# Linear attention and channel mix on one core: the fourth batch's q and the fifth batch's y turned by DMA, loads held behind turning DMAs, and another order table

## The chip, the cores and the metric

The kernel runs on one core of a Trainium2 chip. Its time is device time in microseconds, the median of several runs. Batches are counted from 0 here, as in the code: the fourth batch of q is batch 3, the fifth batch of y is batch 4.

## What is computed

For each of 8 batches and 8 heads of 576 tokens and 64 dimensions: `kv = k^T v`, `out = q kv`, each row of `out` divided by its root mean square and multiplied by `g_norm`. The heads side by side are `x`, 576 x 512 a batch, and then comes a channel mix:

```python
x_prev = x shifted by one token (zeros ahead)
xk = mu_k * x + (1 - mu_k) * x_prev
xr = mu_r * x + (1 - mu_r) * x_prev
k = relu(xk @ w_k)            # 512 x 1024
v = (k * k) @ w_v             # 1024 x 512
out = sigmoid(xr @ w_r) * v   # w_r 512 x 512
```

Inputs and the output are float32; the kernel works in bfloat16 with float32 sums.

## The kernel before, in words

Nothing is scheduled by a compiler. `ORDER` (lines 18 to 110) is a table of words, one step each, and the loop at line 791 records them in this order; every engine runs its own instructions in the order in which the words give them. A word names an operation, batch and part; `'` puts an evacuation or copy on VectorE (DVE) instead of ScalarE (ACT); digits behind `=` choose the PSUM banks. The table has eight periods; period 2 begins with batch 2's `K` steps, and so on.

The steps that matter here, per batch `a`:

- `ld.n.a` (line 189): the load of k, v or q (n = 0, 1, 2), issued by GpSimd (POOL) with a cast to bfloat16, 0.59 MB in SBUF. Odd batches use buffers `in_k`, `in_v`, `in_q`; even ones reuse `sq`, `qT` and `q` of batch 0. Batches 0 and 1 and the weights are loaded ahead of the table (lines 182 to 213 and 689 to 691), batch 1's in two halves.
- `kv.a` (line 278): 72 matmuls on TensorE (PE). `kvo.a` evacuates them. For batch 1 the two halves of the heads are separate words with an `h`: `kvh.0` and `kvh.1` at line 522, `kvho`, `uh`, `sqh`, `redh`, `rsh`, `mulh`, and for the turning back `x0h`, `xh` and `x0ho`, `xho`.
- q has to stand with its dimensions on the partitions. Either `qt.a.0` and `qt.a.1` (line 322) turn it with 72 transposes on PE, and four `qto` evacuate them; or `qd.a` (line 299) issues one transposing DMA on SyncE's (SP's) queue. `QD = 4` (line 293): batches 4 to 7 take the DMA. After a DMA the product `u.a` uses line 316 (`u_turned`) with a second copy of `kv` whose halves are swapped (`kvs.a`), otherwise line 352.
- `sq`, `red`, `nw`, `mul`: squares on ACT, sums and a root by Newton steps on DVE, the product with it on DVE. `nw.a` has 8 small steps.
- y has to be turned back to channels on partitions. Either `x0.a` and `x.a.0.4` (line 435, 36 transposes on PE), evacuated by `x0o` and `xo` with a multiplication by g; or `mul` writes into the single tile `yd`, `yd.a` (line 407) issues one transposing DMA on SP's queue into `xT`, and `gx.a.0`, `gx.a.1` multiply by g in place. `YD = (5, 6, 7)` (line 390).
- `wrap`, `dif`, `sc`, `add`: the token shift and the mix; `add.a.0.*` completes `xk`, `add.a.1.*` completes `xr`.
- `K.a.fc.h` (line 631): four matmuls of 288 columns and a relu into `rt`; `ks` squares it into `sqk`. For batches 0 and 1 these are `Ka`, `Kz`, `Kp` and `ksp`.
- `R.b.t` (line 653): four matmuls of 512 columns and a sigmoid. `V.b.t.part` (line 663): four matmuls of 512 columns; `Vq` is a half of that, two matmuls, with part 0 to 3. R, V and the steps after them go over a pair of batches in 9 tiles of 128 tokens, t = 0 to 8.
- `fin.b.t` (line 676): DVE's product of the two, then two stores on SP's queue. `fip` and `sta` split the stores of the last tiles over SP's and ACT's queues. `L.part` (line 671): the last tile in two column halves.
- `wm.n`: n matmuls on zeros whose result is not used. `tab`: the load of ACT's table with the sigmoid.

Buffers: `work` tiles of one tag rotate (`rt` has 7 places, `sig` 6, `out` 7).

Of the kernel before, what the change touches and what calls it, by code (L numbers as in the profile page):

```python
# [9 lines left out]
FP32 = mybir.dt.float32  # L10
# [9 lines left out]
    cast.0' cast.1' kvc.0.2=01 kvco.1' kvco.0 qtc.0.2=23 qtco.1' cols=4 qtco.0 wm.1.0=1 uc.1=5 sqc.1 uc.0=6  # L20
    qtc.2.2=70 qtco.3' msc.1=1 sqc.0 msc.0=3 qtco.2' rsc.1 wm.1.1=0 kvc.2.1=4 kvco.2 wm.1.2=1 uc.4=2 rsc.0 mcc.1
    uc.2=0 wm.1.3=5 kvc.3.1=7 mcc.0 sqc.2 kvco.3' sqc.4 difh.0.0.256.576 sc.0.0.1.256.576' msc.2=1 uc.3=4
    sc.0.0.0.256.576' uc.5=5 sqc.3 msc.4=3 wm.1.4=7 msc.3=6 rsc.2 add.0.0.0.256.576 wm.1.5=7 Ka.0.4=7 Ka.0.5=1
    rsc.3 mcc.2 mcc.3 dih.0.2.256.576 dih.0.3.256.576 sqc.5 rsc.4 Ka.0.3=6 msc.5=0 fu.0.0.2.256.576 Ka.0.2=4
# [13 lines left out]
    mulh.1.0.1 Vq.0.0.0=3 xho.2.2.1.1 mulh.1.1.1 Vq.0.0.1 xho.2.2.1.0 dif.1.384.576 sc.1.0.2.384.576'
    sc.1.0.1.384.576' Vq.0.0.2 sc.1.0.3.384.576 Vq.0.0.3 sc.1.0.0.384.576' adda.1.0.384.576 xh.0.2.1=07
    xho.0.2.1.1' x0h.1=46 x0ho.1.1' xho.0.2.1.0 wrap.1 x0ho.1.0 dif.1.0.384 sc.1.0.3.0.384' Vq.0.3.3  # L40
    sc.1.0.0.0.384' ld.1.3 Vq.0.1.3 tab sc.1.1.3' R.0.1=0 fin.0.1 Kp.1.0.3=4 Kp.1.0.2=7 sc.1.0.2.0.384'
    add.1.0.1.0.384 Kp.1.0.0'=6 sc.1.1.1 Kp.1.0.1'=0 R.0.0=4 sc.1.0.1.0.384' add.1.0.0.0.384 ld.0.3 R.0.2=7
    kv.2=26 ksp.1.0.0.8 fin.0.0 Kp.1.1.2=4 Kp.1.1.0=0 Kp.1.1.5=7 kvo.2.0 sc.1.1.0' Kp.1.1.1=3 qt.2.1=40
    sc.1.1.2' ksp.1.1.0.2 kvo.2.1 add.1.1.0 qto.2.1.1 qt.2.0=72 R.0.3=3 qto.2.0.1' add.1.1.1 Kp.1.1.3=2
    Kp.1.1.6=6 qto.2.1.0' qto.2.0.0' fin.0.2 fin.0.3 u.2.0=40 sq.2.0.1 ksp.1.1.2.4' Kp.1.1.4'=7 u.2.2=3 u.2.1=25
    sq.2.0.0 sq.2.2.0 sq.2.1.1 red.2.5.9 sq.2.1.0 red.2.0.5 Kp.1.1.7=6 ksp.1.1.4.6 nw.2.0.1 nw.2.1.2 R.1.6=1
    nw.2.2.3 nw.2.3.4 nw.2.4.5 ld.2.4 R.1.7=7 ld.0.4 nw.2.5.6 nw.2.6.7 nw.2.7.8 R.1.8=6 mul.2.0.1 mul.2.2.0
# [8 lines left out]
    K.2.0.1'=5 K.2.1.1=2 K.2.3.1=6 sq.3.0.1 add.2.1.1 red.3.0.5 red.3.5.9 nw.3.0.1 nw.3.1.2 nw.3.2.3 K.2.6.0=5
    nw.3.3.4 R.2.1=2 ld.2.6 R.2.3=6 nw.3.4.5 K.2.1.0=5 K.2.3.0=2 V.1.8.0=6 nw.3.5.6 nw.3.6.7 K.2.6.1=5 V.1.8.1
    ks.2.1 nw.3.7.8 mul.3.1.0 K.2.5.0=2 mul.3.1.1 mul.3.0.1 mul.3.0.0 mul.3.2.0 K.2.2.0=5 K.2.0.0=1 kv.4=02
    ks.2.0' kvo.4.0 fin.1.8 x.3.0.4=75 x0.3=41 K.2.7.0=3 K.2.5.1=0 kvo.4.1 ks.2.2 ks.2.3' x0o.3.1' xo.3.0.4.1'
    kvs.4.1' R.2.2=6 wrap.3 K.2.4.1=1 xo.3.0.4.0' x0o.3.0' dif.3 sc.3.0.3' sc.3.0.2' sc.3.1.2' K.2.4.0=3 ld.0.6  # L60
# [7 lines left out]
    K.3.0.0=2 nw.4.4.5 K.3.5.1=6 ks.3.4 ld.1.7 nw.4.5.6 kvs.5.0' nw.4.6.7 nw.4.7.8 R.3.6=7 K.3.1.0=2 K.3.0.1=6
    K.3.1.1=7 kvs.5.1' ks.3.5 mul.4.1.0 ks.3.2 mul.4.0.0 K.3.6.1=2 K.3.3.1=6 mul.4.2.0 mul.4.1.1 R.3.7=7
    V.2.3.0=3 mul.4.0.1 ks.3.6' ks.3.0 V.2.3.1 ks.3.3' ks.3.1 x0.4=40 fin.2.3 x0o.4.0 x.4.0.4=25 u.5.2=6  # L70
    u.5.1=71 x0o.4.1' xo.4.0.4.1' u.5.0=43 xo.4.0.4.0 V.3.6.0=0 sq.5.0.1 sq.5.0.0 sq.5.2.0 wrap.4 sq.5.1.0 dif.4
    sc.4.0.3 V.3.6.1 fin.3.6 red.5.5.9 sq.5.1.1 red.5.0.5 V.3.5.0=5 R.3.5=2 nw.5.0.1 nw.5.1.2 sc.4.0.0 qd.6
# [14 lines left out]
    add.5.1.0 K.5.3.1=6 K.5.4.1=1 nw.6.7.8 K.5.6.0=4 mul.6.0.1 mul.6.2.0 mul.6.1.0 V.4.1.0=6 kv.7=13 kvo.7.1'
    mul.6.0.0 ks.5.5 mul.6.1.1 sc.5.1.2 ks.5.0 kvo.7.0' K.5.7.1=4 kvs.7.1' K.5.2.0=0 kvs.7.0' ks.5.2 yd.6
    ks.5.3' sc.5.1.3 ks.5.4 V.4.1.1 V.4.3.0=7 ks.5.1' u.7.2=3 u.7.0=54 u.7.1=20 V.4.3.1 ks.5.6' sq.7.0.0
    add.5.1.1 sq.7.0.1 sq.7.2.0 fin.4.1 sq.7.1.0 sq.7.1.1 fin.4.3 K.5.7.0=1 ks.5.7' red.7.0.5 R.5.5=6 R.5.8=7  # L90
    red.7.5.9 R.5.4=1 nw.7.0.1 nw.7.1.2 R.5.7=6 V.5.7.0=7 V.5.8.0=1 nw.7.2.3 nw.7.3.4 gx.6.1' nw.7.4.5 nw.7.5.6
# [734 lines left out]
```

## Time and profile before

| | us |
|---|---|
| median of 3 runs (198.97 to 199.28) | 199.24 |
| the profiled execution, its own time | 198.45 |
| its span, first to last instruction | 196.7 |
| TensorE busy | 185.8 |
| DVE busy | 163.0 |
| ACT busy | 134.1 |
| POOL busy | 27.6 |

The span is what the profile's tables are measured in; the profiled execution's own time has 1.75 us more around it. The transposing DMAs before the change, as SP issued them: q of batch 4 at 63.0, of batch 5 at 77.1, of batch 6 at 103.6 and of batch 7 at 118.9; y of batch 5 at 111.9, of batch 6 at 135.4 and of batch 7 at 149.8. POOL issued the loads of batch 3 from 28.6 to 31.3, of batch 4 from 46.3 to 48.5, of batch 5 from 57.7 to 59.9, of batch 6 from 75.4 to 77.6 and of batch 7 from 92.0 to 94.3.

How to read it: a line of a group or of the timeline gives start or busy time, engine, line of the kernel, what is written and read, and in square brackets how long the engine stood idle before it and what ended that. A window gives the busy time of each engine in a stretch, in the order PE, PEld (weight loads), DVE, ACT, POOL, then the granted share of TensorE's clock, the share of the 16 DMA engines, and GB/s.

### The profile page before, as it was taken

How to read it: one execution, taken by the hardware profiler on the slowest of the kernel's cores; microseconds unless marked ns; L12 is line 12 of the kernel's file. 1: busy time of each engine (PE TensorE's matmuls, PEld its weight loads, DVE VectorE, ACT ScalarE, POOL GpSimd, SP SyncE). 2: the span in 40 equal slices, each digit the busy share in tenths (PEclk: the TensorE clock that was granted, in tenths of full speed). 3: DMA queues.
4: the chain of work that ended last, by engine and by line, in shares of the span. 5: the costliest groups of instructions: out<-in, count | busy, mean ns of one | idle time of the engine just before them, and what ended most of it. 6: DMA issues, size and time to landing. Idle time of an engine off the chain costs nothing.

```text
span 196.7 us, 5776 instructions
## 1 busy us (share of the span) xinstructions
PE 185.8 (94%) x2387; PEld 111.1 (56%) x2409; DVE 163.0 (83%) x356; ACT 134.1 (68%) x275; POOL 27.6 (14%) x44
## 2 busy tenths in 40 slices
PE   7788899999999999999999999999999999999991
PEld 2435565665564667567554775676445666764450
DVE  2488899996999999978999899899899997876241
ACT  2375898779969867969987658989855557532310
POOL 7953343004021004002100000000000000000000
PEclk9999999999999999999999999999999999999999
DMA  5999999999999998999999378335723842005654
GB/s 212 219 211 206 202 205 208 207 217 243 230 230 208 220 189 223 224 170 268 154 215 202 81 136 171 86 80 29 176 45 58 182 107 57 0 0 130 140 144 124
DMA packets 38030, 31.51 MB, mean 160 GB/s; under 512 B 18924, under 2 KB 32500, under 8 KB 38004
## 3 DMA queue, kind: packets, MB, share of 16 engines
q0 software_dynamic: 14400, 16.19, 49.3%
q1 hardware_dynamic: 23204, 14.43, 33.5%
q10 hardware_dynamic: 400, 0.52, 0.8%
q8 instruction: 19, 0.31, 0.6%
q14 instruction: 7, 0.06, 0.1%
HBM read 33.56 MB, written 9.44 MB: 219 GB/s over the span
## 4 chain that ended last, share of the span: by engine, by line
PE 80%; DVE 9%; DMA 4%; issue 2%; ACT 2%; SPq 0%; DVEq 0%; POOLq 0%
PE ps_v L663 28%; PE ps_km L631 28%; PE ps_r L653 15%; DMA q<-in_q_dram 3%; PE ps_kv L287 2%; PE ps_u L316 1%; DVE y L420 1%; PE ps_x L435 1%; DMA out_dram<-out_sb 1%; DVE xT L512 1%; DVE out_sb L676 1%; PE ps_u L352 1%; DVE ss L361 1%; DVE sqk L639 1%; PE ps_qt L330 1%
## 5 line engine op out<-in xcount | busy, mean ns | idle before, releaser
L663 PE MATMUL ps_v<-wv_sb,sqk 128*128 128x512 bf16 x266 | 64.8, 379 | 1.0 <-issue 0.3
L631 PE MATMUL ps_km<-xk,wk_sb 128*128 128x288 bf16 (+3 forms) x480 | 64.0, 285 | 0.0
L631 PEld LDWEIGHTS <-wk_sb 128*128 128x128 bf16 x480 | 45.7, 98 | 16.2
L663 PEld LDWEIGHTS <-sqk 128*128 128x128 bf16 x280 | 26.7, 98 | 29.5 <-issue 0.6
L623 ACT ACTIVATE rt<-ps_km 128x288 bf16<-128x288 f32 (+3 forms) x81 | 33.5, 427 | 12.6 <-PE ps_km L631 9.0
L653 PE MATMUL ps_r<-wr_sb,xr 128*128 128x512 bf16 x136 | 34.9, 379 | 0.5
L656 ACT ACTIVATE sig<-ps_r 128x512 bf16<-128x512 f32 x36 | 21.2, 596 | 18.9 <-PE ps_r L653 18.6
L676 DVE TENSOR_TENSOR out_sb<-ps_v,sig 128x512 f32<-128x512 f32 (+1 forms) x37 | 24.3, 670 | 9.3 <-PE ps_v L663 7.7
L637 ACT ACTIVATE sqk<-rt 128x576 bf16<-128x576 bf16 (+4 forms) x32 | 23.4, 746 | 4.4 <-DVE rt L625 4.2
L601 ACT ACTIVATE m<-dx,cols 128x576 bf16<-128x576 bf16 (+1 forms) x30 | 21.7, 756 | 4.2 <-DVE dx L595 4.0
L625 DVE TENSOR_SCALAR rt<-ps_km 128x288 bf16<-128x288 f32 (+3 forms) x39 | 17.8, 473 | 6.6 <-PE ps_km L631 5.0
L653 PEld LDWEIGHTS <-xr 128*128 128x128 bf16 x144 | 13.9, 98 | 14.2
L361 DVE TENSOR_REDUCE ss<-sq 128x16 f32<-128x1024 bf16 (+1 forms) x12 | 15.8, 1344 | 0.4 <-ACT sq L357 0.4
L357 ACT ACTIVATE sq<-ps_u 128x512 bf16<-128x512 f32 (+1 forms) x30 | 14.6, 556 | 0.0
L618 DVE TENSOR_TENSOR xr<-m,xT 128x1152 bf16<-128x1152 bf16 x16 | 11.9, 750 | 0.8 <-ACT m L601 0.8
L639 DVE TENSOR_TENSOR sqk<-rt 128x576 bf16<-128x576 bf16 (+3 forms) x25 | 11.7, 482 | 0.7 <-ACT rt L623 0.6
L595 DVE TENSOR_TENSOR dx<-xT 128x2304 bf16<-128x2304 bf16 (+5 forms) x13 | 11.4, 893 | 0.4
L603 DVE TENSOR_SCALAR m<-dx,cols 128x576 bf16<-128x576 bf16 (+3 forms) x36 | 11.4, 346 | 0.2
L618 DVE TENSOR_TENSOR xk<-m,xT 128x1152 bf16<-128x1152 bf16 (+2 forms) x16 | 10.9, 699 | 0.2
L420 DVE TENSOR_TENSOR y<-ps_u,rs 128x512 bf16<-128x512 f32 (+1 forms) x15 | 8.4, 628 | 0.1
L217 ACT CAST kv<-ps_kv 128x128 bf16<-128x128 f32 (+1 forms) x15 | 3.3, 244 | 6.9 <-PE ps_kv L472 5.7
L261 PE MATMUL ps_warm<-zeros 128*128 128x512 bf16 x18 | 6.9, 502 | 1.2 <-DVE eps L224 1.2
(91 smaller groups left out, 162.2 us busy)
## 6 DMA issues: line engine op xcount, KB each, us to landing
out_dram<-out_sb SPq DMA_DIRECT2D x67, 128.0 KB, 3.2
qT<-in_v_dram POOLq DMA_DIRECT2D x3, 576.0 KB, 14.4
sq<-in_k_dram POOLq DMA_DIRECT2D x3, 576.0 KB, 12.9
q<-in_q_dram POOLq DMA_DIRECT2D x3, 576.0 KB, 10.8
in_q<-in_q_dram POOLq DMA_DIRECT2D x3, 576.0 KB, 7.9
in_v<-in_v_dram POOLq DMA_DIRECT2D x3, 576.0 KB, 14.3
in_k<-in_k_dram POOLq DMA_DIRECT2D x3, 576.0 KB, 11.8
wk_sb<-in_moe_w_k_dram POOLq DMA_DIRECT2D x2, 512.0 KB, 9.1
```

What stands on the lines that cost most here:

```text
L357: ACT.activation(out=sq[:, rg(t0, n, i) if n else slice(0, 1)], in_=held["u", a, part, i][1], func=AF.Square)
L361: DVE.tensor_reduce(out=ss[:, g0:g1], in_=sq[:, g0:g1], op=ALU.add, axis=AX.X)
L601: eng.activation(out=out_, in_=in_, func=AF.Copy, scale=mu)
L618: DVE.tensor_add(out=dst, in0=m[:, hs, c0:c1], in1=x[:, hs, c0:c1])
L623: eng.activation(out=dst, in_=ps, func=AF.Relu)
L625: eng.tensor_scalar(out=dst, in0=ps, scalar1=0.0, scalar2=None, op0=ALU.max)
L631: nc.tensor.matmul(ps[:, n, :], wk_sb[:, cc, 128 * fc:128 * fc + 128], at[b]["xk"][:, cc, c0:c1], start=(cc == 0), stop=(cc == NHP - 1))
L637: eng.activation(out=sqk[:, fcs, o:o + n], in_=src, func=AF.Square)
L653: nc.tensor.matmul(ps, xr[:, cc, 128 * t:128 * t + 128], wr_sb[:, cc, :], start=(cc == 0), stop=(cc == NHP - 1))
L656: ACT.activation(out=sig[b, t], in_=give("r"), func=AF.Sigmoid)
L663: nc.tensor.matmul(ps, sqk[:, fc, 128 * t:128 * t + 128], wv_sb[:, fc, :], start=(fc == 0), stop=(fc == NFC - 1))
L676: DVE.tensor_mul(out=o, in0=give(key), in1=sig[b, t][:, c])
```

## The change

`QD` becomes 3 and `YD` becomes (4, 5, 6, 7): batch 3's q and batch 4's y are turned by DMA, the transposes, evacuations and the straight product for them go, and `kvs.3`, `qd.3`, `yd.4` and `gx.4` come. Each transposing DMA leaves a mark in a list, and the next load of the table first lets POOL copy two elements of the turned tile, which waits until that DMA has landed. The loads' order changes a little (v of batch 6 ahead of its q, q of batch 7 last). The buffers `rt`, `sig` and `out` are given out from lists of free places, and tiles of odd and even batches get names of their own, one buffer each. The last tile is cut into 384 and 128 columns, and `L.1` (128 columns) comes first. The whole table `ORDER` is another one; the core of it is below: the end of the opening with the first part of period 1, and pieces of periods 1 to 3 around batches 3 and 4.

```diff
-    qt.1.0=50 Kz.0.3' fu.0.0.0.0.256 qto.1.0.1 Kz.0.7 ksp.0.0.0.4' qto.1.0.0' kvh.0=41 kvho.0.0 Kp.0.1.1'=3
-    kvho.0.1 Kp.0.1.0'=2 uh.1.0=60 ksp.0.0.4.8 sqh.1.0.0 uh.0.0=74 ld.1.2 uh.2.0=1 sqh.0.1.0 ksp.0.1.0.4'
-    sqh.0.0.0 sqh.1.1.0 ld.0.2 sqh.2.0.0 redh.5.9.0 Kp.0.1.2=5 redh.0.5.0 rsh.5.9.0 mulh.0.0.0 Kp.0.1.3=3
-    rsh.0.5.0 Vq.0.1.0=2 mulh.0.1.0 ld.2.2 Vq.0.1.1 ksp.0.1.4.8 sc.0.1.3' mulh.2.0.0 Vq.0.2.0=5 qt.1.1=37
-    xh.2.2.0=41 mulh.1.1.0 Vq.0.2.1 xho.2.2.0.0 qto.1.1.1' mulh.1.0.0 qto.1.1.0' xho.2.2.0.1 kvh.1=07 kvho.1.1'
-    x0h.0=46 kvho.1.0 x0ho.0.1 x0ho.0.0' xh.0.2.0=13 uh.0.1=07 xho.0.2.0.1' uh.1.1=46 xho.0.2.0.0' sqh.0.0.1
-    sqh.0.1.1 uh.2.1=3
...
+    fu.0.0.3.0.256 Kz.0.5 Kz.0.6 fu.0.0.2.0.256 Kz.0.1 qt.1.0=60 qto.1.0.0 qto.1.0.1 Ka.0.7=1 Kz.0.7' kvh.0=47
+    ld.0.2 kvho.0.1' kvho.0.0 uh.1.0=53 uh.0.0=26 uh.2.0=0 ksp.0.0.4.8' sqh.1.0.0 sqh.1.1.0 sqh.2.0.0
+    ksp.0.0.0.4' redh.0.5.0 Kp.0.1.2=1 rsh.0.5.0 sqh.0.1.0 mulh.2.0.0 sqh.0.0.0
     """,
     """
+    mulh.1.0.0 Kp.0.1.1=4 Kp.0.1.0=7 x0h.0=10 mulh.1.1.0 redh.5.9.0 xh.0.2.0=53 rsh.5.9.0 Kp.0.1.3=4 sc.0.1.3'
+    xho.0.2.0.0' sc.0.1.1' ld.1.2 mulh.0.0.0 qt.1.1=75 mulh.0.1.0 xh.2.2.0=24 xho.2.2.0.1 x0ho.0.0' kvh.1=61
+    ld.2.2 qto.1.1.1' ksp.0.1.0.4' qto.1.1.0' xho.0.2.0.1 kvho.1.1' xho.2.2.0.0' kvho.1.0 Vq.0.0.0=5 uh.2.1=4
+    uh.1.1=37 x0ho.0.1' uh.0.1=61 ksp.0.1.4.8' ld.2.3 ld.1.3 sqh.2.0.1 Vq.0.2.0=2 add.0.1.1 Vq.0.0.1
...
+    qto.2.0.1 qt.2.1=41 ld.2.4 qto.2.1.1 Kp.1.0.1=0 add.1.0.1.0.384 fin.0.0 qd.3 Kp.1.1.6=3 sc.1.1.0 qto.2.1.0'
...
+    add.2.1.1 qd.4 V.1.7.1 R.1.6=1 V.1.6.1 kv.4=24 fin.1.7 u.3.2=6 kvo.4.0 u.3.1=35 add.2.0.1 u.3.0=71 sc.2.1.1'
...
+    sc.3.1.0' V.2.2.0=7 sc.3.0.3 sc.3.0.0' sc.3.0.2 sc.3.0.1' ld.0.6 qd.5 V.2.1.1 V.2.2.1 kv.5=25 u.4.0=60
+    fin.2.1 sc.3.1.2 kvo.5.0 sq.4.0.0 u.4.1=41 add.3.0.0 sq.4.0.1 u.4.2=3 sq.4.2.0 sq.4.1.1 sq.4.1.0 add.3.0.1
...
+    mul.4.2.0 K.3.3.1=6 ks.3.3 K.3.1.0=4 mul.4.1.1 K.3.1.1=2 mul.4.0.1 K.3.5.0=3 yd.4 ld.0.7 K.3.0.1=6 K.3.0.0=1
...
-    V.7.4.1 sta.7.5 V.7.7.0=4 fin.7.4 V.7.7.1 sta.7.6 fip.7.7 sta.7.7 L.0=2 L.1=6
+    fip.7.7 V.7.5.1 fip.7.5 sta.7.7 sta.7.6 sta.7.5 L.1=6 L.0=2
...
+        while turning:
+            nc.gpsimd.tensor_copy(out=passed, in_=turning.pop())
         nc.gpsimd.dma_start(out=x_in[name, b], in_=by_token(dram[name], b))
 
-    def gate(a):
-
-        nc.gpsimd.tensor_copy(out=passed, in_=at[a]["qT"][0:1, G - 1:G + 1, 0])
+    turning = []
...
-            at[a][key] = work.tile(shape, dtype, tag=tag or key, name=tag or key)
+            name = f"{tag or key}{key[1] if tag else a % 2}_"
+            at[a][key] = work.tile(shape, dtype, tag=name, name=name, bufs=1)
...
-    QD = 4
+    QD = 3
...
         nc.sync.dma_start_transpose(out=qT_, in_=x_in["q", a].rearrange("p m x -> p (m x)"))
+        turning.append(qT_[0:1, 0, 0:2])
...
-    YD = (5, 6, 7)
+    YD = (4, 5, 6, 7)
...
+        turning.append(xT[a % 2][0:1, 0:2, 0])
...
+    free = {"rt": list(range(7)), "sig": list(range(6)), "out": list(range(7))}
+    place = {}
+
+    def slot(kind, key, shape, dtype):
+
+        n = place[kind, key] = free[kind].pop(0)
+        return work.tile(shape, dtype, tag=f"{kind}{n}_", name=f"{kind}{n}_", bufs=1)
+
+    def leave(kind, key):
+        free[kind].append(place.pop((kind, key)))
...
-        c = slice(C // 2 * part, C // 2 * part + C // 2)
+        c = (slice(0, 3 * C // 4), slice(3 * C // 4, C))[part]
```

More of the change, by code (lines that the diff above doesn't have):

```diff
@@ L19 @@
     """
[L20 to L24, printed above, removed]
@@ L38 @@
[L38 to L42, printed above, removed]
@@ L43 @@
[L43 to L47, printed above, removed]
@@ L56 @@
[L56 to L60, printed above, removed]
@@ L68 @@
[L68 to L72, printed above, removed]
@@ L87 @@
[L87 to L91, printed above, removed]
@@ new lines @@
+    ld.2.2 qto.1.1.1' ksp.0.1.0.4' qto.1.1.0' xho.0.2.0.1 kvho.1.1' xho.2.2.0.0' kvho.1.0 Vq.0.0.0=5 uh.2.1=4
+    uh.1.1=37 x0ho.0.1' sqh.1.1.1 uh.0.1=61 ksp.0.1.4.8' ld.2.3 ld.1.3 sqh.2.0.1 Vq.0.2.0=2 add.0.1.1 Vq.0.0.1
+    Vq.0.1.0=0 sqh.1.0.1 Vq.0.2.1 sqh.0.1.1 sqh.0.0.1 redh.0.5.1 ld.0.3 redh.5.9.1 rsh.0.5.1 Vq.0.1.1 Vq.0.1.2
+    mulh.2.0.1 Vq.0.2.2 mulh.1.0.1 x0h.1=43 Vq.0.0.2 mulh.1.1.1 rsh.5.9.1 Vq.0.1.3 x0ho.1.0 mulh.0.1.1 tab
+    mulh.0.0.1 xh.0.2.1=71 xh.2.2.1=46 xho.2.2.1.1' xho.0.2.1.1' xho.2.2.1.0 add.0.1.0 Vq.0.2.3 dif.1.384.576
@@ new lines @@
+    qto.2.0.0' ksp.1.0.0.8' Kp.1.1.3=5 Vq.0.3.3 u.2.0=14 Kp.1.1.2=0 sq.2.0.1 add.1.1.0 Kp.1.1.1=7 sq.2.0.0
+    Kp.1.1.0=3 fin.0.2 Kp.1.1.5=5 Kp.1.1.4=2 u.2.1=07 ksp.1.1.2.4' u.2.2=3 sq.2.1.1 sq.2.1.0 red.2.5.9 sq.2.2.0
+    Kp.1.1.7=5 fin.0.3 ksp.1.1.4.6' red.2.0.5 nw.2.0.1 nw.2.1.2 nw.2.2.3 ld.2.5 R.1.5=2 ksp.1.1.0.2 nw.2.3.4
+    R.1.7=6 nw.2.4.5 nw.2.5.6 nw.2.6.7 nw.2.7.8 mul.2.1.0 R.1.4=5 ksp.1.1.6.8 mul.2.2.0 mul.2.1.1 R.1.8=2
+    mul.2.0.1 mul.2.0.0 V.1.5.0=6 V.1.8.0=5 V.1.5.1 fin.1.5 kv.3=03 x0.2=27 x.2.0.4=41 V.1.4.0=6 x0o.2.1
@@ L654, in r @@
                              start=(cc == 0), stop=(cc == NHP - 1))
-        sig[b, t] = work.tile([128, C], BF16, tag="sig", name="sig", bufs=6)
+        sig[b, t] = slot("sig", (b, t), [128, C], BF16)
         ACT.activation(out=sig[b, t], in_=give("r"), func=AF.Sigmoid)
@@ L674, in finish @@
     def finish(b, t, key, c=slice(0, C), queues=(nc.sync, nc.sync)):
-        o = outs[b, t] = work.tile([128, c.stop - c.start], FP32, tag="out", name="out_sb", bufs=7)
+        o = outs[b, t, c.start] = slot("out", (b, t, c.start), [128, c.stop - c.start], FP32)
         DVE.tensor_mul(out=o, in0=give(key), in1=sig[b, t][:, c])
@@ L678, in finish @@
             store(b, t, i, q_, c)
+        if c.stop - c.start == C:
+            leave("sig", (b, t))
     outs = {}
@@ L683, in store @@
         bb, j = b - b % 2 + (2 * t + i) // G, (2 * t + i) % G
-        q_.dma_start(out=out[bb].rearrange("(p j) c -> j p c", j=G)[j, :, c], in_=outs[b, t][half(i), :])
+        q_.dma_start(out=out[bb].rearrange("(p j) c -> j p c", j=G)[j, :, c], in_=outs[b, t, c.start][half(i), :])
+        if i == 1:
+            leave("out", (b, t, c.start))
     PARTS0 = ((4 * P, S), (0, 4 * P))
```

95 lines of the change are left out of this document (55 added, 40 removed).

## The prediction

> **What bounds the kernel now.** I read the page's table of engines first, then its chain that ended last, and then busy time by stage.
>
> ```profile
> PE 185.8 (94%) x2387; PEld 111.1 (56%) x2409; DVE 163.0 (83%) x356; ACT 134.1 (68%) x275; POOL 27.6 (14%) x44
> ...
> PE 80%; DVE 9%; DMA 4%; issue 2%; ACT 2%; SPq 0%; DVEq 0%; POOLq 0%
> ```
>
> TensorE (PE) is busy for 94% of the span and is 80% of the chain; its granted clock is full in every slice. The next view is busy time by window, cut where TensorE meets the first matmul of a stage (the second column is PE's busy time in the stretch, the fourth DVE's):
>
> ```profile
> 21.87:28.99 7.12, 6.89 (x138) 5.02 (x141) 6.79 (x15) 6.01 (x16) 2.58 (x4) 1.00 1.22 204
> 28.99:30.48 1.49, 1.49 (x66) 1.29 (x67) 1.46 (x7) 1.22 (x6) 1.04 (x2) 1.00 1.25 211
> 30.48:64.00 33.52, 33.13 (x536) 18.50 (x538) 30.71 (x68) 28.02 (x57) 5.28 (x8) 1.00 1.20 221
> 64.00:83.60 19.60, 19.34 (x314) 12.52 (x316) 18.52 (x39) 15.49 (x36) 2.23 (x3) 1.00 1.13 214
> 83.60:108.90 25.30, 25.02 (x319) 14.93 (x320) 22.88 (x48) 21.12 (x45) 2.23 (x3) 1.00 1.15 203
> 108.90:125.30 16.40, 16.29 (x239) 10.59 (x240) 15.22 (x32) 12.19 (x27) 0.00 (x0) 1.00 0.60 122
> 125.30:151.30 26.00, 25.68 (x281) 14.93 (x284) 24.21 (x53) 20.94 (x41) 0.00 (x0) 1.00 0.40 70
> ```
>
> From 30.48 us to the end of the last matmul at 192.4 TensorE idles about 1.6 us in all. So a matmul taken out there is worth its own time, and a wait put in there costs its own time; there is almost no idle time to win back. DVE comes close behind (2.4 us idle of 25.3 in the fifth row). The DMA engines are full up to 110 us (the last two columns: share over 1, some 200 to 220 GB/s).
>
> **Transposes taken off TensorE.** The chain in order of time has the operations that go, and the one that replaces a product:
>
> ```profile
> 56.71 0.65 PE ps_qt L330 x72
> ...
> 64.87 0.81 PE ps_u L352 x40
> ...
> 74.85 0.63 PE ps_x L435 x36
> ...
> 136.49 0.78 PE ps_u L316 x68
> ```
>
> Batch 3's q turns (72 transposes) cost 0.65. The 36 that turn batch 4's y are shown by batch 3's of the same form: 0.63. The product of batch 3 goes from line 352 (0.81) to line 316 (0.78). Together TensorE does 0.65 + 0.63 + 0.03 = **1.3 us less**. On ACT and DVE four evacuations of batch 3's q (0.45 to 0.65 each) and four of batch 4's y (0.3 to 1.1 each) go; two half copies (0.2 to 0.4 each), two scalings by g (1.25 each on ACT, both there by the new table) and 0.45 more in batch 4's multiplies come. They lie beside TensorE, so I count them at nothing, apart from the DVE point below.
>
> **The opening of the new table.** The load list ahead of the table is unchanged, and the DMA engines are full from 4 us on, so I take its landings as they are. The second half of batch 1's v is issued at 15.27 and takes 13.4 us to land: 28.7. `kvh.1` needs it; TensorE runs in order, so nothing written behind `kvh.1` can start before that. `kvh.0` waits for the first half in the same way (issued 9.78, 12.0 to land: 21.8). The timeline of TensorE between the two:
>
> ```profile
> 21.90 0.48 PE L522 MATMUL ps_kv<-in_v,in_k 64*64 64x64 bf16 x36 [0.37 <-ACT qT L217]
> 22.31 1.92 PE L631 MATMUL ps_km<-xk,wk_sb 128*128 128x256 bf16 x16
> 24.16 0.59 PE L540 MATMUL ps_u<-kv,qT 64*128 64x64 bf16 x20
> 24.68 1.92 PE L631 MATMUL ps_km<-xk,wk_sb 128*128 128x256 bf16 x16
> 26.43 1.46 PE L663 MATMUL ps_v<-wv_sb,sqk 128*128 128x512 bf16 x5
> ...
> 28.99 0.48 PE L522 MATMUL ps_kv<-in_v,in_k 64*64 64x64 bf16 x36
> ```
>
> Before, this stretch holds four half-steps `Vq` (eight matmuls of 512 columns; four take 0.86, so 1.73), and it is full: 6.89 busy of 7.12. The new table puts all four behind `kvh.1` and brings only `x0h.0` and `xh.0.2.0` forward (0.4). That leaves 6.89 - 1.73 + 0.4 = 5.56 of work for a stretch of at least 28.70 - 21.87 = 6.83. So 1.73 - 0.4 = 1.33 of work slips behind `kvh.1`, which can start at most 0.29 earlier than before: a loss of **1.0 at least**. Then comes `Vq.0.0.0`, which needs the square `ksp.0.1.0.4'`. In DVE's new list that is the sixteenth step from `kvho.0.1'` on (22.4 us, the end of `kvh.0`): 0.2 + two squares of 0.82 + reductions 1.4 + five multiplies 1.9 + two scalings 0.7 + evacuations 0.35, 0.24, 0.44 + its own 0.69 = 7.6, so 30.0; with the overlap of ends that the timeline shows (starts some 0.08 closer than durations) 28.7. `kvh.1` ends at about 29.2, so TensorE waits 0 to 0.8, and the products after it wait for one more evacuation. Bounds of the whole opening: 1.0 to 2.1. I take **1.5**, the middle, since DVE's starts before show overlaps in part only. Other pieces of the opening (four more warm-up matmuls) lie in waits for the weights (1.04 and 0.23 us) and cost nothing; without that cover they would cost 0.32 each.
>
> **Late transposing DMAs.** In the queue's own waits POOL's next q load already stood behind a transposing DMA before the change (15.5 and 14.4 us). The first was issued at 63.01 and its waiter went at 75.39, 12.4 later; the second 77.10 and 92.04, 14.9. Each ended some 1.9 after the last of the three loads queued beside it had landed (73.4 and 90.2, issue plus time to landing). Batch 3's new one cannot start before its q lands (28.63 + 17.4 = 46.0) and has five loads beside it, the last of which lands at 62.7 before the change, plus about 2 for the transposing DMA's own share: it ends at 58 by the first measure, 66.6 by the second. The product `u.3` that needs it comes on TensorE at 64.00 (old start of the third period) + 0.71 (`kv.4`) + 1.73 (`V.1.8`) - 0.65 + 1.5 = 67.3. It just fits, so 0 in the sum, and up to 3 for the range. The other holds: loads of batches 5 to 7 go out some 5 to 7 us later than before; `kv.5` to `kv.7` come 4 us or more behind the latest landing I get that way, so nothing. The copy of two elements on POOL has no row; POOL's small MEMSETs take 0.1 to 0.3, and POOL has only loads behind it. Below nothing is excluded: no load is late now.
>
> [...]
>
> **DVE between batch 3 and batch 4.** From `add.3.0` to `add.4.0` the new list gives DVE all five multiplies of batch 5 (4 x 0.68 + 0.86) and more small steps, and takes out three finishes (0.68 each) and two evacuations (0.74 and 0.27); summed by rows it is 25.7 where it was 23.0. TensorE's list for the stretch grows by 1.0. DVE's spare time shrinks from 2.4 to 2.4 - 2.7 + 1.0 = 0.7. If DVE's old idle time came back whole, it would cost 1.7. I take **0.3**.
>
> **The end.** Line 671 becomes 128 columns, then 384, for 256 twice (0.119 us a matmul before; 512 columns take 0.215). By length the sum is the same; if 128 columns take as long as a weight load (98 ns), it is 0.2 more. The last multiply grows from 0.42 toward 0.69: +0.13. The last store is 96 KB, between 64 KB (2.2 us) and 128 KB (2.6 to 3.2): +0.2. Together 0.1 to 0.8; I take **0.4**.
>
> **Sum.** -1.3 + 1.5 + 0.3 + 0.4 = +0.9 on the profiled execution's own 198.45 (span 196.7 and 1.75 around it): 199.35. That execution lies 0.79 under the median of the runs, 199.24, so the forecast is 199.24 + 0.9 = **200.1 us**. A measurement of this kernel tells about 0.2% (0.4 us) from no change.
>
> **Rivals.**
> - *The opening's gap is small and the transposes' time stays won* (faster). The opening costs its least, 1.0, the end 0, DVE nothing, and the new order closes 0.4 of the 1.6 us of idle time: 199.24 - 1.3 + 1.0 - 0.4 = 198.5. For it: the whole 1.3 is on the chain. Against it: `kvh.1`'s landing. It decides if v lands earlier than 28.4; with no opening loss at all it would be 197.9.
> - *The transposing DMA replaces the transposes as the wait.* If batch 3's keeps only the share of the DMA engines that the second one had (three loads took 13.4 us of its 14.9) and five loads slow it in proportion, it ends at 46 + 14.9 x 5/3 = 70.8 against 67.3, and TensorE waits up to 3.5 at `u.3`. With half of that: 200.1 + 1.7 = 201.8. For it: the two rows above. Against it: it can start some 20 us before the earliest need (46.0 against 67.3 - 1.5).
> - *DVE becomes the bound* before batch 4 and again at batch 6 (24.21 busy of 26.00 before): 200.1 + 1.4 = 201.5.
> - *The holds hold nothing*: q loads wait for the same DMAs anyway. True for two of them before; the time is then the forecast's.
>
> **How the numbers follow.** Forecast 0.50 (own range 199.3 to 200.9), faster rival 0.25, late DMA 0.17, DVE 0.08; the last rival is inside the first. Faster by over 0.2% (under 198.84): 0.20 from the faster rival. Within 0.2%: 0.12 of the forecast, 0.05 of the faster rival, 0.01 of the late DMA: 0.18. Slower: the rest, 0.62. The range reaches from the faster rival's 198.5, less a little, to the late DMA's 201.8, plus a little: 198.3 to 202.2, with about one in ten left out on each side.
>
> **What would show it.** TensorE's 72 + 36 transposes of batches 3 and 4 gone; a gap of over 1 us on TensorE ahead of the second line-522 group, and a second gap before the first line-663 matmul; no wait for `qT` at batch 3's product; DVE idle under 1 us between the two adds; the last matmul at about 193. The forecast is wrong if `kvh.1` starts much before 28.7, if TensorE waits for a transposing DMA, or if the gap in the opening is won back by idle time that I count as lost.

## The result, and the profile after

The changed kernel took 202.21 us in the median of four runs (200.75 to 205.54), the kernel before 199.11 beside it: 1.0149 times as long, 95% interval 1.0104 to 1.0194. A second series of six runs gave 200.99 (200.39 to 202.07) against 198.84: 1.0110 (1.0082 to 1.0138). The ratios here and below count the runs within 1.5% of the fastest of their kernel. So it is slower by 2 to 3 us where 0.9 was forecast; the first median lies at the very end of the recorded range (198.3 to 202.2), the second inside it. The first profiled execution was the longest of its four (205.54); why executions differ is part of what follows, so both profiles are shown.

The table of engines, the granted clock in 40 slices and the chain of the first profile (execution of 205.54, span 203.8):

```profile
PE 188.7 (93%) x2317; PEld 111.3 (55%) x2337; DVE 160.6 (79%) x351; ACT 132.3 (65%) x277; POOL 29.2 (14%) x50
...
PEclk9999999999999999999999999969999999999999
...
PE 76%; DVE 4%; ACT 3%; issue 3%
```

The 108 transposes are gone (2317 matmuls with some records missing, 2337 in the second profile), TensorE still leads the chain, but a slice of the clock row reads 6, and "issue", time in which an engine waited for nothing that the profile shows, has 3%. TensorE's timeline of this profile has it in two places (square brackets: idle time before the row, and its releaser):

```profile
87.44 0.81 PE L675 MATMUL ps_v<-wv_sb,sqk 128*128 128x512 bf16 x3
90.16 0.38 PE L675 MATMUL ps_v<-wv_sb,sqk 128*128 128x512 bf16 x1 [1.91 <-issue]
...
127.38 1.88 PE L633 MATMUL ps_km<-xk__2827,wk_sb 128*128 128x288 bf16 x14
131.59 5.02 PE L633 MATMUL ps_km<-xk__2827,wk_sb 128*128 128x288 bf16 x26 [2.33 <-issue]
```

Each gap lies inside one step, between matmuls with the same operands, so no data can be missing. Busy time by window behind the second gap (seventh column: granted clock; sixth: POOL):

```profile
130.00:132.00 2.00, 0.41 (x4) 0.33 (x4) 0.07 (x1) 0.00 (x0) 0.00 (x0) 1.00 0.08 24
132.00:134.00 2.00, 2.00 (x13) 1.37 (x12) 0.46 (x1) 1.79 (x4) 0.00 (x0) 0.69 0.70 70
134.00:136.00 2.00, 2.00 (x11) 1.21 (x9) 1.78 (x8) 0.53 (x2) 0.00 (x0) 0.50 0.92 138
```

The clock falls to a half for 3.4 us once the matmuls go on, and four K steps take 0.34 to 0.47 more each: 1.7 us.

What comes late, as the experiments below show, is TensorE's own code. The DMA queues have one of kind "instruction" (q8) that brings packets of 16 KB, 18 in this profile. In the stretch from 77.0 to 87.8 the list of queues has none:

```profile
q1 hardware_dynamic: 4574, 1.61, 74.9%
q0 software_dynamic: 635, 0.69, 37.2%
```

and from 87.8 to 88.9, when the gap has begun, there is one:

```profile
q8 instruction: 1, 0.02, 5.6%
```

The second profile (execution of 200.57, span 198.8) has gaps at the same two instructions, of 0.60 and 0.71 us, and the clock stays full:

```profile
88.41 0.38 PE L675 MATMUL ps_v<-wv_sb,sqk 128*128 128x512 bf16 x1 [0.60 <-issue]
...
128.19 2.00 PE L633 MATMUL ps_km<-xk__2827,wk_sb 128*128 128x288 bf16 x15 [0.71 <-issue]
```

Its opening and batch 3's product:

```profile
21.62 0.48 PE L524 MATMUL ps_kv<-in_v,in_k 64*64 64x64 bf16 x36 [0.40 <-DMA in_v<-in_v_dram]
22.41 0.86 PE L542 MATMUL ps_u<-kv__491,qT__444 64*128 64x64 bf16 x20 [0.31 <-ACT kv__491 L216]
...
28.65 0.48 PE L524 MATMUL ps_kv<-in_v,in_k 64*64 64x64 bf16 x36
29.48 0.60 PE L675 MATMUL ps_v<-wv_sb,sqk 128*128 128x512 bf16 x2 [0.35 <-DVE sqk L641]
...
66.74 0.93 PE L287 MATMUL ps_kv<-qT,sq 64*64 64x64 bf16 x72
67.48 1.18 PE L317 MATMUL ps_u<-kv__1293,qT__1103 64*64 64x64 bf16 x72
```

The product at 67.48 has no bracket: it waited for nothing. Where the time went follows from TensorE's timeline read word by word: the time from the first weight load of a word to that of the next, summed by kind. The table gives the second profile less the profile before:

| words | us |
|---|---|
| opening: kvh +0.52, msc +0.53, uh +0.34, xh +0.60, warm-ups -0.68, others -0.06 | +1.25 |
| qt, x, x0 (-1.34), products u (+0.27), kv (-0.06) | -1.13 |
| K, V, R: the two gaps | +1.31 |
| K, V, R: the rest | +0.51 |
| TensorE's end (192.42, then 194.36) | +1.94 |
| from there to the end of the span (4.28, then 4.44) | +0.16 |

### The profile page after: what moved, and what is told of

The parts are those of the page before. It is cut to its first block, busy times and chain, and to the rows that moved or that the text cites. A ratio compares the mean times of both kernels' runs of the same rounds, so it can differ in the third digit from the quotient of the medians.

```text
span 203.8 us, 5658 instructions
## 1 busy us (share of the span) xinstructions
PE 188.7 (93%) x2317; PEld 111.3 (55%) x2337; DVE 160.6 (79%) x351; ACT 132.3 (65%) x277; POOL 29.2 (14%) x50
## 4 chain that ended last, share of the span: by engine, by line
PE 76%; DVE 4%; ACT 3%; issue 3%
PE ps_v L675 29%; PE ps_km L633 27%; PE ps_r L665 14%; PE ps_kv L287 2%; PE ps_u L317 2%; ACT sq__1641 L358 1%; PE ps_v L683 1%; PE ps_x L437 1%; DVE y__579 L562 1%; DVE ss__564 L552 1%; ACT kv__1481 L216 1%; DVE sqk L641 1%; DVE xk__966 L620 1%; DVE rt L627 1%; PE ps_u L353 0%
## 5 line engine op out<-in xcount | busy, mean ns | idle before, releaser
L633 PEld LDWEIGHTS <-wk_sb 128*128 128x128 bf16 x480 | 46.5, 99 | 20.1 <-issue 3.1
L633 PE MATMUL ps_km<-xk__2827,wk_sb 128*128 128x288 bf16 x64 | 10.2, 321 | 2.3 <-issue 2.3
L625 ACT ACTIVATE rt<-ps_km 128x384 bf16<-128x384 f32 (+2 forms) x18 | 8.5, 504 | 3.1 <-PE ps_km L633 1.9
L633 PE MATMUL ps_km<-xk__2039,wk_sb 128*128 128x288 bf16 x64 | 9.0, 286 | 0.0
L633 PE MATMUL ps_km<-xk__1604,wk_sb 128*128 128x288 bf16 x64 | 8.7, 286 | 0.2 <-ACT rt__1671 L625 0.2
L633 PE MATMUL ps_km<-xk__966,wk_sb 128*128 128x192 bf16 (+1 forms) x64 | 8.5, 286 | 0.3 <-DVE rt L627 0.3
L633 PE MATMUL ps_km<-xk__2502,wk_sb 128*128 128x288 bf16 x64 | 8.7, 286 | 0.0
L633 PE MATMUL ps_km<-xk__3223,wk_sb 128*128 128x288 bf16 x64 | 8.7, 286 | 0.0
L633 PE MATMUL ps_km<-xk__3385,wk_sb 128*128 128x288 bf16 x64 | 8.5, 286 | 0.0
L427 ACT ACTIVATE xT<-ps_x,cols 128x256 bf16<-128x256 bf16 (+3 forms) x8 | 4.6, 600 | 3.7 <-PE ps_x L437 3.6
L427 ACT ACTIVATE xT<-xT,cols 128x1152 bf16<-128x1152 bf16 x5 | 6.1, 1247 | 0.0
L724 PE MATMUL ps_km<-xk__365,wk_sb 128*128 128x320 bf16 x32 | 5.5, 298 | 0.4 <-DVE xk__365 L609 0.2
L260 PEld LDWEIGHTS <-zeros 128*128 128x128 bf16 x22 | 2.5, 122 | 4.8 <-issue 2.9
L641 DVE TENSOR_TENSOR sqk<-rt 128x1280 bf16<-128x1280 bf16 (+3 forms) x7 | 5.0, 722 | 0.1
L429 DVE TENSOR_SCALAR xT<-ps_x,cols 128x256 bf16<-128x256 bf16 (+3 forms) x12 | 4.1, 368 | 0.8 <-PE ps_x L437 0.8
L724 PEld LDWEIGHTS <-wk_sb 128*128 128x128 bf16 x32 | 3.0, 97 | 2.6 <-issue 1.4
## 6 DMA issues: line engine op xcount, KB each, us to landing
in_q<-in_q_dram POOLq DMA_DIRECT2D x3, 576.0 KB, 10.9
```

The source lines that it names most:

```text
L260: nc.tensor.matmul(ps, zeros[:, :128], zeros, start=True, stop=True)
L427: eng.activation(out=dst, in_=src, func=AF.Copy, scale=g_sb)
L429: eng.tensor_scalar(out=dst, in0=src, scalar1=g_sb, scalar2=None, op0=ALU.mult)
L625: eng.activation(out=dst, in_=ps, func=AF.Relu)
L633: nc.tensor.matmul(ps[:, n, :], wk_sb[:, cc, 128 * fc:128 * fc + 128], at[b]["xk"][:, cc, c0:c1], start=(cc == 0), stop=(cc == NHP - 1))
L641: eng.tensor_mul(out=sqk[:, fcs, o:o + n], in0=src, in1=src)
```

## The experiments

All times are medians in us; the kernel before ran beside each of these kernels, and its median is given with them. A gap "without a releaser" is one that the profile puts down to "issue".

**The changed kernel again.** No edit.

> The changed kernel once more, nothing edited, with a fresh profile. In its first profile TensorE stood for 2.0 us (87.9 to 90.2) and 2.5 us (inside a K step, 128.7 to 131.6) with nothing that the profile shows to wait for, each time just as a 16 KB instruction packet of TensorE's came later than usual, and the granted clock fell behind the second gap (1.7 us more). Theory (instructions come late behind transposing DMAs): at least one such gap again, at a late instruction packet, with its size free to differ from run to run; median 200.5 to 203. Rival (the gaps were a disturbance of that one execution): no gap over 0.6 us without a releaser, and a median of 199.5 to 200.5, near the sum of the prediction.

200.99 against 198.84. Gaps of 0.60 and 0.71 us at the same instructions. They belong to the kernel and not to one execution; their length varies.

**Batch 5's transposing DMA later.**

```diff
-ld.0.6 qd.5 V.2.1.1 V.2.2.1 kv.5=25 u.4.0=60 ... u.4.2=3 sq.4.2.0
+ld.0.6 V.2.1.1 V.2.2.1 kv.5=25 u.4.0=60 ... u.4.2=3 qd.5 sq.4.2.0
```

> The changed kernel with one word moved: the transposing DMA of batch 5's q, qd.5, stands behind the products of batch 4 (u.4.2) instead of ahead of kv.5 and u.4, so it is issued some 3 us later. kv.5 and u.4 are 72 and 68 matmuls that last 10 ns or so each: TensorE uses up instructions fastest there. Theory (its packets held TensorE's instruction packet back): the gap near 88 goes or is under 0.5 us, the second gap near 129 stays, and the time falls by 0.5 to 2.0 us against the changed kernel. Rival (the gap has another cause, or the delay only moves on with the DMA): the gap is there still, within 5 us of the old place, and the time is the same within 0.4 us.

207.11 against 198.84, ratio 1.0411 (1.0380 to 1.0442). The gap near 88 went, as the theory had it, and so did the one near 129, which it had staying; but 6 us came in their place, which neither theory nor rival foresaw. TensorE's waits:

```profile
PE ps_u L317 <- DMA qT__2049<-in_q: 6.2, 1, 6.2
```

SP started the transposing DMA at 84.98 where it had been 81.08, 4 us later, and POOL issued batch 6's three loads (84.5 to 86.7) beside it; SP needed 10.9 us to issue it instead of 3.4. Started 3 us ahead of the three loads it held nothing up; started with them it made the product that needs it 6 us late.

**The old order with the half-steps behind `kvh.1`.** The kernel before, with one move:

```diff
-rsh.0.5.0 Vq.0.1.0=2 mulh.0.1.0 ld.2.2 Vq.0.1.1 ... Vq.0.2.0=5 ... Vq.0.2.1 ... kvh.1=07 kvho.1.1'
+rsh.0.5.0 mulh.0.1.0 ld.2.2 ... kvh.1=07 Vq.0.1.0=2 Vq.0.1.1 Vq.0.2.0=5 Vq.0.2.1 kvho.1.1'
```

> The kernel before with one edit: the four half-steps Vq.0.1.0, Vq.0.1.1, Vq.0.2.0 and Vq.0.2.1 stand behind kvh.1, as the new table has them, instead of ahead of it. It prices the opening alone. Theory (the opening's term of the prediction's sum): TensorE stands for 1.2 to 1.5 us ahead of kvh.1 (1.73 of work leaves a stretch that was full, less the 0.29 by which kvh.1 can start earlier), and the time is 1.0 to 1.5 us longer than before. Rival (the gap is won back by later idle time): the gap is there, and the time is within 0.4 us of before.

200.33 against 198.84, ratio 1.0087 (1.0054 to 1.0120): 1.5 us, the upper end. TensorE's waits show where it stands, ahead of `qt.1.1` and of `kvh.1`:

```profile
PE ps_qt L330 <- DMA in_q<-in_q_dram: 1.8, 2, 1.3
...
PE ps_kv L522 <- DMA in_v<-in_v_dram: 0.8, 1, 0.8
```

Nothing behind it wins the gap back. It isn't the price of the move alone: `kvh.1` started at 29.72, 0.7 later than before, since in this profile the second half of v landed at 29.58 and not at 28.70.

**No holds.** The changed kernel without

```diff
-        while turning:
-            nc.gpsimd.tensor_copy(out=passed, in_=turning.pop())
```

> The changed kernel without the copies on POOL that hold the loads behind the transposing DMAs, with nothing else edited. Theory (instructions late behind dense DMA packets): the holds are no cause; loads then run beside the transposing DMAs, these take longer, TensorE may wait for one (batch 5's y or batch 3's q), and the time is the same or up to 2 us longer than the changed kernel. Rival (the holds cost the time, by bunching the loads behind each transposing DMA): the gaps near 88 and 129 go and the time falls by 1 us or more.

210.98 against 198.84, ratio 1.0617 (1.0583 to 1.0650). TensorE's waits:

```profile
PE ps_v L673 <- DVE yd L398: 7.0, 1, 7.0
PE ps_u L315 <- DMA qT__1463<-q: 2.7, 1, 2.7
```

v of batch 6 and all of batch 7 go out 15 to 23 us earlier and share the queues with the transposing DMAs: q of batch 4 comes 2.7 us late, and y of batch 4 holds `yd` from batch 5's multiplies for 7. The holds do what the change says, and much more than nothing. The direction was the theory's; the size was five times the most it allowed.

**Where the instruction packets begin: 32 and 96 short matmuls.** The first warm-up, ahead of all work, with 32 (with 96 it is `warm(8)` and `range(96)`):

```diff
-    warm(12)
+    warm(11)
+    short = [take(("short", e), [128, HD], FP32, "ps_short") for e in range(2)]
+    for n in range(32):
+        e, i = n // 2 % 2, n % 2
+        nc.tensor.matmul(short[e][half(i), :], zeros[half(e), :HD], zeros[half(e), :HD], start=True, stop=True)
+    for e in range(2):
+        give(("short", e))
```

> The changed kernel with 32 short matmuls on zeros (64 columns, 64x64) in the first warm-up, ahead of all work, in place of one of its twelve wide ones: 62 instructions more on TensorE, about the same time there, no result used, nothing else touched. Theory: TensorE's instructions come in packets of 16 KB, one per some 255 instructions, each asked for as one runs out and 2 to 5 us on its way while the DMA queues are full. Stretches with kv and u next to each other use 255 up in some 2 us. 62 instructions shift where the packets begin, so that by the times of the last run three packets begin at the start of such a stretch (near 67, 84 and 120 us) and must be used up in 2 to 4 us: gaps without a releaser of 1 us or more at two or three of these, and the time 2 to 8 us longer than the changed kernel. Rival (the gaps come from the DMAs or the table and not from the instructions): gaps of 0.5 to 1 us at the old places, 200.5 to 201.5 us, as the changed kernel.

> The same with 96 short matmuls in place of four wide ones: 184 instructions more on TensorE ahead of all work. By the times of the last run no packet of instructions would then have to be used up in less than 7 us. Theory: no gap without a releaser over 0.3 us, although the DMAs, the holds and the table stay as they are, and the time is 1.0 to 1.8 us shorter than the changed kernel (199.2 to 200.0). Rival: the gaps of 0.6 and 0.7 us at the old places, 200.5 to 201.5 us.

With 32 the runs took 210.9 to 216.8, median 215.00, before 198.67. Its waits:

```profile
PE ps_km L633 <- issue: 4.9, 2, 4.1
PE ps_r L665 <- issue: 2.7, 1, 2.7
PE ps_u L317 <- issue: 2.4, 1, 2.4
```

Gaps of 4.06, 2.38 and 2.71 us at 70, 92 and 133 us (the theory's 67, 84 and 120, later by what was lost before), one more of 0.82 at 46, and a halved clock behind three of them: the three places were foreseen, the total (some 14 us) was not. Thirty-two matmuls on zeros, of some 0.5 us (96 took 1.49), in place of one wide one and where TensorE waits anyway (0.3 us for `rt`, with the 32 and in the second profile), make the kernel 14 us slower, and of what follows nothing but the position of the instructions has changed. That settles it against the rival.

With 96 there is no gap without a releaser, as the theory had it, and yet 201.50 against 198.67 (ratio 1.0145, 1.0117 to 1.0174). The first packet now came at 9.37 us, into the first loads, and one of the loads of batch 0's v landed at 11.40 instead of 10.22:

```profile
PE ps_kv L474 <- DMA rt<-in_v_dram: 1.2, 1, 1.2
```

`kvh.1` came 1.31 later than in the changed kernel, batch 7's product at the same 138.72: what the gaps had cost was won, and lost again in the opening.

**The short matmuls later.** 32 and 64 of them (the word `ws.n` records n as above) in place of the warm-ups `wm.2.4` and `wm.4.5`:

```diff
-sqc.3 wm.2.4=5 msc.3=1 rsc.4 mcc.2 dih.0.2.256.576 wm.4.5=4
+sqc.3 ws.32=54 msc.3=1 rsc.4 mcc.2 dih.0.2.256.576 ws.64=45
```

> As the run with 96 short matmuls, but these stand in the place of the two warm-ups of two and four wide matmuls that wait for w_k at 13 to 15 us (32 and 64 short ones), so that no packet of instructions meets the first loads: in that run one at 9.4 us did, v's third load landed 1.2 us later, and the whole opening came 1.3 us later, which took back what the gaps' going had won. Theory (the gaps cost the changed kernel 1.3 us): no gap without a releaser over 0.3 us, the opening as in the changed kernel, 199.4 to 200.0. Rival (the DMA queues' pace sets the time, and TensorE only waits elsewhere): waits for batch 5's k or batch 4's q or y come in their place, and 200.5 to 201.2.

The seven runs spread from 199.32 to 205.27, median 202.52 against 198.73: the expected 199.4 to 200.0 was missed. (The ratio, 1.0076, 1.0044 to 1.0107, rests on the three shortest.) In the profile of one of these three the opening is as in the changed kernel and both old gaps are gone, but a new one stands inside batch 2's transposes:

```profile
PE ps_qt L339 <- issue: 1.1, 1, 1.1
```

What held up the four longer runs wasn't profiled. The shortest execution, 199.32, and the profiled ones with their gaps taken off (200.57 - 1.31, 200.56 - 1.09) give an estimate of 199.3 to 199.5 for the change without late code: some 0.6 over the median before, 1.0 over its shortest run (198.29).

**The old opening on the new table.** Words up to `tab` from the table before, then the new ones:

```diff
-    uh.1.1=37 x0ho.0.1' sqh.1.1.1 uh.0.1=61 ... tab ... Vq.0.3.2 wrap.1 x0ho.1.1' R.0.1=4 ...
+    uh.1.1=13 xho.0.2.0.0' ... sc.1.0.0.0.384' ld.1.3 Vq.0.1.3 tab ld.0.3 R.0.1=4 R.0.0=1 sc.1.1.2' ...
```

> The changed kernel, but its table begins with the words of the table before, up to the load of ACT's table with the sigmoid (PSUM banks renamed to fit), and goes on with the new words; what the two have in another order there is done once. So the opening is the old one, and batch 3's q and batch 4's y, the holds, the loads from batch 3 on and the last tile are as in the change. Theory (the opening costs what TensorE's time word by word showed: kvh, msc, uh and xh 2.0 more, warm-ups 0.7 less, so 1.2): 1.0 to 1.5 us shorter than the changed kernel, some 199.8, with the two gaps without a releaser still there. Rival (the late transposing DMA decides): batch 3's product comes 1.2 us earlier and meets the transposing DMA that ended 1.7 us ahead of it; TensorE waits there for up to 1 us and the gain is under 0.7.

201.18 against 198.67, ratio 1.0131 (1.0101 to 1.0160): no gain, although in the profile both gaps without a releaser are gone too (none over 0.3). So the rival stands, though not at batch 3's product: it came 1.3 earlier, at 66.18, and just met its transposing DMA, behind which POOL's copy went at 66.19. TensorE's timeline:

```profile
83.00 0.78 PE L284 MATMUL ps_kv<-in_v,in_k 64*64 64x64 bf16 x72 [0.87 <-DMA in_k<-in_k_dram]
84.22 0.87 PE L314 MATMUL ps_u<-kv__1477,qT__1460 64*64 64x64 bf16 x72 [0.44 <-DMA qT__1460<-q]
```

and 0.9 more at 104.6 for batch 4's y. Batch 5's k landed at 82.96, in the changed kernel at 81.94: the loads did not come earlier when TensorE did. These three waits, 2.2 us, are about what the opening (1.2) and the gaps (1.3) had cost. The DMA queues are a second bound just under TensorE, and the opening's cost and theirs overlap.

**The last tile in two halves.**

```diff
-        c = (slice(0, 3 * C // 4), slice(3 * C // 4, C))[part]
+        c = slice(C // 2 * part, C // 2 * part + C // 2)
```

with `L.0` first.

> The changed kernel with the last tile cut into 256 and 256 columns again, the lower half first, as before. Theory of the prediction (the 384-column end costs 0.4): 0.3 to 0.5 us shorter. From the traces (TensorE needs 2.12 us for the last tile in both cuts, and what follows TensorE's end is 4.44 us where it was 4.28): 0.1 to 0.2 us shorter, which cannot be told from no change.

201.11 against 198.67 (ratio 1.0128, 1.0102 to 1.0153), which the time alone can't tell from the changed kernel. In the trace TensorE needs 2.12 us in either cut, and 4.40 us follow its end instead of 4.44: the cut is worth under 0.1.

**One part undone, both undone.** q of batch 3 by TensorE again (`QD = 4`; `qt.3.0`, `qt.3.1` and their evacuations behind batch 2's flip, with `ld.2.5` behind them), and y of batch 4 as well (`YD = (5, 6, 7)`, `x0.4` and `x.4.0.4` where `yd.4` stood):

```diff
-fin.0.0 qd.3 Kp.1.1.6=3 ... ld.2.5 ... ld.1.5 x0o.2.0' wrap.2 ... dif.2 V.1.7.0=7 ... kvs.3.1 ... kvs.3.0
+fin.0.0 Kp.1.1.6=3 ... x0o.2.0' qt.3.0=41 qto.3.0.0 qto.3.0.1 qt.3.1=20 ld.2.5 ld.1.5 wrap.2 ... dif.2 qto.3.1.1' qto.3.1.0' V.1.7.0=7
```

> The changed kernel with one part undone: batch 3's q is turned by TensorE again (72 transposes behind batch 2's flip, four evacuations), no qd.3, no hold behind it, the straight product; batch 4's y stays with the DMA and the table is else as it is. TensorE has 0.62 more. Its packets of instructions begin elsewhere, and the gap near 88 should go (0.6 to 1.4). Theory (qd.3 cost only that gap): 200.5 to 201.3. Rival (qd.3 also takes the DMA queues' time that the loads of batch 5 and 6 lack): batch 5's last load, which landed at 82 to 83, lands 4 us or more earlier, and the time is 199.8 to 200.4.

> Both parts undone: q of batch 3 and y of batch 4 are turned by TensorE, as before; what is left of the change is the table (with its opening), the holds, the places by list and the last tile. Theory (the opening costs 1.2, the end 0.16, the rest nothing, and there are no gaps without a releaser, since the packets of instructions begin elsewhere): 200.0 to 200.5 against some 198.8 before. Rival (the new order of K, V and R costs as well): over 200.8. Rival (the opening's cost is won back behind it): under 199.4.

> The old opening, q of batch 3 by TensorE, y of batch 4 by the DMA, the new order behind it: the parts of the change that should win something without the one that loads the DMA queues earliest. Theory: before (198.7) less the 36 transposes of batch 4's y (0.6), and the end 0.16: 198.0 to 198.6, if no packet of instructions comes late. Rival (y's DMA is the wait, as the 0.9 us at 104.6 in the run with the old opening): a wait for xT or yd of 0.5 us or more, 199.0 to 199.8.

205.24 (1.0294, 1.0262 to 1.0326), 204.35 (1.0294, 1.0262 to 1.0325) and 211.02 (1.0603, 1.0565 to 1.0641), against 198.73. All three expectations failed, in the main for one reason: these changes move the places at which packets begin. The timeline with q by TensorE, of its longest execution (212.96; five of the seven took 203.6 to 205.3):

```profile
63.34 3.61 PE L675 MATMUL ps_v<-wv_sb,sqk 128*128 128x512 bf16 x16 [0.78 <-issue]
...
72.22 0.29 PE L353 MATMUL ps_u<-kv__1288,qT__1417 64*128 64x64 bf16 x8 [2.25 <-issue]
...
92.29 0.45 PE L317 MATMUL ps_u<-kv__1557,qT__1540 64*64 64x64 bf16 x25 [1.83 <-issue]
...
133.37 0.22 PE L317 MATMUL ps_u<-kv__2446,qT__2439 64*64 64x64 bf16 x2 [3.46 <-issue]
```

8.3 us of gaps, and the clock halved behind some; with the old opening besides 0.9, 1.7, 2.5 and 3.6 us at 62, 68, 87 and 127. The loads did come earlier with q by TensorE (batch 5's last at 79.61), as the rival had it, but its time can't be read under the gaps. The table alone has two gaps, 1.15 and 1.71, and three words at half clock (1.48 more); its profiled execution, 205.48, is 201.1 without them, 0.6 above the theory's upper end and where the rival has it by which the new order of K, V and R costs as well; that stays untested. The expectations had counted the transposes that come back, and not that the straight product of batch 3 has 40 matmuls where the other has 72: they were 64 instructions off in where the packets begin.

**The gaps side by side.** The table has the number of weight loads and matmuls that the trace has ahead of the matmul that ends a gap, for each gap of over 0.5 us without a releaser, and the time from the start of the last 16 KB packet ahead of it to that matmul:

| kernel | instructions ahead | us from packet to matmul |
|---|---|---|
| changed, second profile | 2737, 3759 | 2.42, 2.32 |
| 32 short | 1459, 2225, 2737, 3759 | 2.33, 2.41, 2.36, 2.37 |
| 96 short, later | 1461 | 2.29 |
| last tile 256 | 2737 | 2.20 |
| q of 3 by TensorE | 1971, 2227, 2737, 3759 | 2.24, 2.28, 2.45, 2.34 |
| table alone | 1971, 2228 | 2.23, 2.22 |
| old opening, q by TensorE | 1975, 2229, 2741, 3763 | 2.32, 2.38, 2.33, 2.28 |

Whatever the steps are, TensorE stops at 1460, 1972, 2228, 2738 or 3760 instructions: steps of 256, to within the few that are no matmul or weight load. With those few counted in (11 to 19, recorded in the same two rows of the profile), every gap of the table begins behind 1473, 1985, 2241, 2753 or 3777 instructions, exact multiples of 256 apart. And TensorE goes on 2.2 to 2.45 us after its packet has started; in the twelve profiles that lack no records, no such block of 256 begins sooner after its packet. Both are the mark of code that is used up before the next 16 KB are there.

Counting back 256 from a gap tells when TensorE entered the block before it. In the second profile that was 83.8 for the first gap: 256 instructions were used up by 87.8, in 4.0 us, and the packet started 2.2 us after the entry. For the second it was 120.6: the block lasted 6.9 us, but the packet started only 5.3 us after the entry. So the first gap is more a matter of fast use and the second of a late packet. When a packet is asked for, no trace shows: "as one runs out" was the author's estimate.

None of these versions beats the kernel before.

## Why the prediction was right and wrong

It forecast the direction and, on the profiled execution's own time, +0.9; measured are +2.1 in the second profile and 2 to 3 in the medians. The medians lie inside the range or at its end by luck: the range reaches so far up for late transposing DMAs, which was not what happened, and the opening, DVE and the end were set 0.8 too high together, which hid part of the 1.8 that the sum does not have at all (the gaps and K, V, R).

- **Transposes off TensorE**, -1.3: right for the transposes, -1.34. The product of batch 3, counted at 0.78 and 0.03 cheaper than before, was busy for 1.18; with it the products and kv took 0.21 back, so the term comes to -1.13.
- **The opening**, +1.5 (1.0 to 2.1): right in mechanism and nearly in size, +1.25 in the words, and 1.5 when done alone, part of it a later landing of v. `kvh.1` started at 28.55 in the second profile and 29.16 in the first (28.7 forecast), and the gap ahead of it was not one of over 1 us but a thinner TensorE all the way from 21.6: 6.38 busy of 7.03. `Vq.0.0.0` waited 0.35 for its square (0 to 0.8 forecast). The step failed where it treats the opening as a cost of its own: with the old opening back, the DMA queues take the time.
- **Late transposing DMAs**, 0, "just fits": right for batch 3. It had landed by 66.0 (66.6 by the second measure; the last of the five loads beside it landed at 65.4), the product came at 67.5 (67.3). "`kv.5` to `kv.7` come 4 us or more behind the latest landing" failed for `kv.5`: 1.6 us (81.94, 83.55), and batch 4's product 0.8. POOL's timeline shows what holds them:

```profile
66.00 0.18 POOL L194 COPY passed<-qT__1103 1x2 bf16<-1x2 bf16 x1 [20.36 <-DMA qT__1103<-in_q]
...
83.33 0.18 POOL L194 COPY passed<-qT__1464 1x2 bf16<-1x2 bf16 x1 [14.86 <-DMA qT__1464<-q]
```

  Loads of batches 5 and 6 landed 8.5 and 9 us later than before (73.4 and 90.2, then 81.9 and 99.2). The rival on late DMAs was not what happened, but it is 0.8 to 1.5 us away, as moving one word by 4 us showed.
- **How long batch 3's transposing DMA took**: 19 us from issue (47.1) to landing beside five loads, where the two rows that the step started from have 12.4 and 14.9. The plain load of the same size issued at 44.9 took 20.5 us beside it.
- **DVE**, +0.3: nothing found; it idles 1.23 us between the two adds (under 1 forecast) and TensorE waits for none of it.
- **The end**, +0.4: mis-sized, 0.16, and the cut itself under 0.1.
- **What failed** is the step under "What bounds the kernel now": "there is almost no idle time to win back", and so only the work and the listed waits count. It left out TensorE's supply of code. In the kernel before, that came in time at every packet (no such wait of a matmul over 0.2 us). The new table sets `kv.5` right ahead of `u.4`, and `u.6` around `kv.7`: 288 matmuls and weight loads in 1.5 us, more than a packet holds, while the transposing DMA and the loads fill the queues. The gaps come behind these (`u.4` ends at 85.2 and the gap begins at 87.8; `u.6` and `kv.7` end at 121.6, and the gap begins at 127.5). That cost 1.3 us in the second profile, and 5.9 with the clock in the first (1.91 + 2.33 + 1.7). Such a stretch alone is not enough. The kernel before has a denser one at 56 us (`kv.3`, `qt.3` and transposes of y), with the DMA engines as full:

```profile
56.00:58.00 2.00, 2.00 (x178) 1.89 (x178) 2.00 (x5) 0.92 (x4) 0.31 (x1) 1.00 1.21 208
```

  These are 356 instructions in 2 us without a wait. Counted as above, a block of 256 begins inside it, at 56.5, and its packet had started 4.7 us earlier. So it is the place at which the packets begin, together with such stretches, that decides, and no step of the prediction asks for it.

Where code came late, the longest gap was 4.06 us (32 short matmuls); where it came in time, as in the kernel before, no such wait was over 0.2.

What stays open: whether keeping kv and u apart in the new table would close the gaps (not tried), how much a packet's delay owes to transposing DMAs and how much to loads, 0.51 us in K, V and R, and 0.6 in the table alone.

## What to carry to other kernels

Read "issue" in the waits and the queue of kind "instruction" before pricing an order of work: where tiny matmuls stood together here (288 matmuls and weight loads in 1.5 us) while the DMA queues were full, TensorE ran out of code for up to 4.06 us, and even another warm-up moved where (with 32 short matmuls in one, the kernel took 14 us more). Try a few paddings and look at all the gaps; spreading such stretches out is the other idea, not tried here. And don't add up what two resources within 1 to 2 us of each other cost: with the old opening, what the opening (1.2) and the gaps (1.3) had cost came back as 2.2 us of waits for DMAs.
